# LayerNorm on GpSimd in another form, and a last output tile in three steps: a fused attention and spatial-gating kernel

## The chip, the cores and the metric

The kernel runs on one core of a Trainium2 chip. The metric is the device time of one execution in microseconds. The profile's span, from first to last instruction, is about 1.8 us shorter (span 203.2 in an execution of 204.99 us). Each execution has a state: "slow" if it is over 1.5% above the fastest of the same kernel. That window keeps very different shares of the executions (8 of 22 in experiment 5, 20 of 22 in experiment 9), so medians of all executions stand beside the ratios. Ratios are computed as the mean time of one kernel's fast runs over that of the other's fast runs of the same rounds, so they are not quite the ratio of the medians that I quote.

In the profile PE is TensorE (PEld its weight loads), DVE VectorE, ACT ScalarE, POOL GpSimd, SP SyncE. L326 is line 326 of that kernel's own source, so the same step has other line numbers in other kernels.

## The reference, cut to what matters

```python
# attention in chunks of 64 tokens: x[8, 576, 512]; then the gated block:
h = np.maximum(x @ w_in, 0.0)                       # 512 -> 1024
u, v = h[..., :512], h[..., 512:]
mu = np.mean(v, axis=-1, keepdims=True)
var = np.mean((v - mu) ** 2, axis=-1, keepdims=True)
v_n = (v - mu) / np.sqrt(var + 1e-06)               # <- the change is here
v_s = np.einsum('ts,bsd->btd', w_spatial, v_n) + b_spatial[None, :, None]
out = (u * v_s) @ w_out                             # <- and at the end of this
```

There are 4608 tokens, that is 36 tiles of 128. Four tiles are shared by two batches: their lower 64 rows (the even half) go one way, their upper 64 rows (the odd half) another. `w_spatial` is drawn very small (0.01/576) beside a bias of ones, so the comparison with the reference hardly feels an error in `v_n`.

## The kernel before

Each step is an `op` with an engine, an assumed duration, the ops it waits for and a function that emits the instructions. A list scheduler with its own clock runs through them while the kernel is built and so fixes the order of instructions on every engine. Each engine then works its list in that order.

```python
def rs(n):                       # ScalarE: rstd = exp(-0.5 ln(var + eps)), for one or two tiles
    ...
    nc.scalar.activation(lnv[:, :w], mvs[n][:, :w, 1:2], AF.Ln, bias=eps_sb)
    nc.scalar.activation(rstds[n][:, :w, 0:1], lnv[:, :w], AF.Exp, scale=-0.5)

def nm(n):                       # VectorE: -mean * rstd, the L311 of the profile
    nc.vector.scalar_tensor_tensor(out=rstds[n][:, :w, 1:2], in0=mvs[n][:, :w, 0:1], scalar=-1.0,
                                   in1=rstds[n][:, :w, 0:1], op0=ALU.mult, op1=ALU.mult)

def vnorm(t):                    # GpSimd: v * rstd + (-mean * rstd), L326 (L322 for an even half)
    ...
    nc.gpsimd.tensor_scalar(vn[t], vr, s[:, 0:1], s[:, 1:2], op0=ALU.mult, op1=ALU.add)

def vnorm_o(t):                  # VectorE: the odd half of a shared tile, L331
    nc.vector.tensor_scalar(y[0:64], vr[64:128], s[64:128, 0:1], s[64:128, 1:2],
                            op0=ALU.mult, op1=ALU.add)
...
op(f"nm{n}", DVE_, 0.17, [f"rs{n}"], lambda n=n: nm(n), 1)
op(f"vn{t}", POOL_, 0.80, [f"nm{n}"], lambda t=t: vnorm(t), 0, [("vn", t)])
...
# last tile in two halves, stored from SyncE's queue
n = 2 if t == NT - 1 else 1
...
op(f"st{w}", SP_, 0.62, [f"eo{w}"], lambda t=t, c=c: store(t, c), -200, dma=(SP_, 0.85 / n, f"st{w}*", 128))
```

GpSimd has a second job: it casts the loaded q, k and v from float32 to bfloat16 (L176, L179), and TensorE waits for those casts.

The softmax here doesn't subtract the row's maximum and nothing guards it: scores larger than these inputs give would overflow.

## Time and profile before

| | before |
|---|---|
| executions known at the prediction (us) | 202.41, 206.48, 208.65, and the profiled one, 204.99 |
| span of the profiled execution | 203.2 us |
| TensorE busy / idle | 192.2 / 11.0 us |
| GpSimd busy | 106.7 us (52%) |

GpSimd's three costliest groups are the normalisations and the casts of v and of q (those of k, 16.6 us, are like those of q). Each line gives the count, then busy us and mean ns of one, then idle us just before them:

```profile
L326 POOL TENSOR_SCALAR vn<-v_relu,rstd 128x512 bf16<-128x512 f32 x32 | 24.4, 781 | 28.7 <-DVE rstd L311 22.3
...
L179 POOL CAST vaug<-vf 128x512 bf16<-128x512 f32 x36 | 21.9, 626 | 15.8 <-issue 8.7
...
L176 POOL CAST qb<-qf 128x1024 bf16<-128x1024 f32 x16 | 16.7, 1042 | 20.8 <-DMA qf<-in_q_dram 19.1
```

### The profile page before, as it was taken

What the parts mean: (1) busy time and instruction counts of PE and PEld (TensorE: products, weight loads), DVE (VectorE), ACT (ScalarE), POOL (GpSimd) and SP (SyncE); (2) the same over time, 40 slices, a digit from 0 to 9 for tenths busy, and PEclk for the clock granted to TensorE, in tenths of its full rate; (3) what the DMA queues carried; (4) which work ended last, traced back from release to release, by engine and by line L of the source; (5) the groups of instructions that cost most, each with busy time, mean ns of one, the idle gap of its engine ahead of it and who ended that gap; (6) DMA issues with size and microseconds to landing.
All of it is one profiled execution on the core that took longest, in us unless ns stands there. A gap on an engine that the chain in (4) does not pass through costs nothing.

```text
span 203.2 us, 7600 instructions
## 1 busy us (share of the span) xinstructions
PE 192.2 (95%) x3228; PEld 107.2 (53%) x3228; DVE 127.6 (63%) x337; ACT 115.5 (57%) x209; POOL 106.7 (52%) x155
## 2 busy tenths in 40 slices
PE   7999978989999999999999988999999999999992
PEld 2344434554765556446645634656665446467651
DVE  3226457797746767877776898754477888327330
ACT  2223637867166777976677774574376861640432
POOL 8789394379962375996774995961102222200000
PEclk9999999999999999999999999999999999999999
DMA  5999979999989998999979999871401400212515
GB/s 155 217 311 227 290 202 173 223 271 199 294 209 337 304 298 218 266 293 285 257 190 279 261 240 305 232 197 55 155 5 62 151 2 3 103 74 84 208 52 206
DMA packets 57218, 40.10 MB, mean 197 GB/s; under 512 B 40864, under 2 KB 44384, under 8 KB 57184
## 3 DMA queue, kind: packets, MB, share of 16 engines
q1 hardware_dynamic: 52368, 36.32, 61.5%
q0 software_dynamic: 4816, 3.29, 11.1%
q8 instruction: 25, 0.41, 0.8%
q14 instruction: 9, 0.07, 0.1%
HBM read 32.79 MB, written 9.44 MB: 208 GB/s over the span
## 4 chain that ended last, share of the span: by engine, by line
PE 88%; DVE 3%; DMA 2%; POOL 2%; ACT 2%; issue 1%; SPq 1%; POOLq 0%; ACTq 0%
PE big L352 20%; PE big L280 16%; PE big L376 15%; PE big L337 15%; PE big L390 6%; PE o_ps L231 4%; PE s_ps L194 4%; PE s_ps L216 3%; PE o_ps L245 2%; DMA qf<-in_q_dram 2%; PE big L194 1%; DVE xT L253 1%; PE big L262 1%; POOL qb L176 1%; PE s_ps L192 1%
## 5 line engine op out<-in xcount | busy, mean ns | idle before, releaser
L369 DVE TENSOR_TENSOR gat<-big,uT 128x288 bf16<-128x288 f32 (+8 forms) x96 | 30.2, 351 | 22.6 <-PE big L352 21.2
L352 PE MATMUL big<-wsf,vn 128*128 128x288 bf16 x256 | 40.4, 286 | 0.0
L280 PE MATMUL big<-w_in_sb,xT 128*128 128x512 bf16 x144 | 37.1, 379 | 3.2 <-DVE xT L253 3.1
L326 POOL TENSOR_SCALAR vn<-v_relu,rstd 128x512 bf16<-128x512 f32 x32 | 24.4, 781 | 28.7 <-DVE rstd L311 22.3
L296 DVE BATCH_NORM_STATS2 bst<-v_relu 128x6 f32<-128x512 f32 x36 | 24.9, 690 | 18.8 <-ACT v_relu L287 18.7
L337 PE MATMUL big<-xT,w_in_sb 128*128 128x512 bf16 x144 | 34.6, 380 | 0.0
L376 PE MATMUL big<-w_out_sb,gat 128*128 128x512 bf16 (+2 forms) x164 | 34.4, 376 | 0.0
L287 ACT ACTIVATE v_relu<-big 128x512 f32<-128x512 f32 x35 | 20.9, 598 | 23.8 <-PE big L280 23.0
L382 ACT COPY o_sb<-big 128x512 f32<-128x512 f32 (+1 forms) x30 | 16.9, 571 | 23.6 <-PE big L376 23.6
L179 POOL CAST vaug<-vf 128x512 bf16<-128x512 f32 x36 | 21.9, 626 | 15.8 <-issue 8.7
L221 ACT ACTIVATE eT<-s_ps 128x512 bf16<-128x512 f32 x36 | 21.5, 597 | 15.4 <-PE s_ps L194 8.8
L199 ACT COPY qkT<-s_ps 128x1024 bf16<-128x1024 bf16 x29 | 29.2, 1007 | 1.7 <-PE s_ps L194 1.5
L352 PEld LDWEIGHTS <-vn 128*128 128x128 bf16 x256 | 24.0, 97 | 8.6
L176 POOL CAST qb<-qf 128x1024 bf16<-128x1024 f32 x16 | 16.7, 1042 | 20.8 <-DMA qf<-in_q_dram 19.1
L239 DVE TENSOR_TENSOR x<-o_ps,rz 128x512 bf16<-128x512 f32 x36 | 24.9, 691 | 1.2
L280 PEld LDWEIGHTS <-xT 128*128 128x128 bf16 x144 | 13.1, 97 | 18.2 <-DVE xT L253 5.2
L376 PEld LDWEIGHTS <-gat 128*128 128x128 bf16 (+1 forms) x164 | 13.5, 100 | 14.9 <-issue 1.5
L337 PEld LDWEIGHTS <-w_in_sb 128*128 128x128 bf16 x144 | 13.1, 98 | 14.7
L287 ACT ACTIVATE uT<-big 128x512 bf16<-128x512 f32 x27 | 16.1, 596 | 7.3 <-PE big L337 7.3
L253 DVE COPY xT<-o_ps 128x512 bf16<-128x512 bf16 x36 | 14.6, 406 | 8.3 <-PE o_ps L245 8.3
L390 PE MATMUL big<-warm 128*128 128x512 bf16 x63 | 18.5, 431 | 1.2 <-DVE warm L394 1.2
L352 PE MATMUL big<-wst,tail 65*128 65x288 bf16 x64 | 18.4, 288 | 0.0
(53 smaller groups left out, 208.6 us busy)
## 6 DMA issues: line engine op xcount, KB each, us to landing
out_dram<-o_sb SPq DMA_DIRECT2D x35, 256.0 KB, 2.1
qf<-in_q_dram SPq DMA_DIRECT2D x32, 256.0 KB, 5.2
kf<-in_k_dram SPq DMA_DIRECT2D x32, 256.0 KB, 4.9
vf<-in_v_dram SPq DMA_DIRECT2D x32, 256.0 KB, 6.0
w_in_sb<-in_moe_w_in_dram POOLq DMA_DIRECT2D x2, 512.0 KB, 8.2
vf<-in_v_dram SPq DMA_DIRECT2D x8, 128.0 KB, 5.7
ws_nat<-in_moe_w_spatial_dram POOLq DMA_DIRECT2D x1, 576.0 KB, 9.5
qb<-in_q_dram POOLq DMA_DIRECT2D x16, 32.0 KB, 5.4
```

Of the source, the lines that this page charges most:

```text
L179: CAST[eng](vaug[t % NVB][:, :, 0:64], f32.pop(("v", t)))
L199: nc.scalar.copy(qkT[n], tr_v.rearrange("p b r x -> p b x r"))
L239: nc.vector.tensor_tensor(xs[t], av_v[:, :, :, 0:64], rz.to_broadcast([128, 2, 4, D]), op=ALU.mult)
L280: nc.tensor.matmul(y, xT[g][:, cb, r * 128:(r + 1) * 128], w_in_sb[:, cb, F:], start=(cb == 0), stop=(cb == 3))
L287: nc.scalar.activation(out_, in_, AF.Relu)
L296: nc.vector.bn_stats(bst, relu[t])
L326: nc.gpsimd.tensor_scalar(vn[t], vr, s[:, 0:1], s[:, 1:2], op0=ALU.mult, op1=ALU.add)
L337: nc.tensor.matmul(y, w_in_sb[:, cb, fb * 128:(fb + 1) * 128], xT[g][:, cb, :], start=(cb == 0), stop=(cb == 3))
L352: nc.tensor.matmul(y[:, 0:HS], lhsT, rhs, start=(i == 0), stop=(i == 4))
L369: nc.vector.tensor_tensor(gat[b][:, db, c:c + n], ps["sp", b, half, db][:, o:o + n], uT[g][:, db, r:r + n], op=ALU.mult)
L376: nc.tensor.matmul(y[r0:r0 + n, c], gat[b][:, jb, s:s + n], w_out_sb[:, jb, c], start=(jb == 0), stop=(jb == 3))
L390: nc.tensor.matmul(y, warm[:, 0:128], warm, start=True, stop=True)
```

## The change

The intent is to drop the 20 small VectorE products and one hop in the chain from statistics to normalised tile, by applying (v - mean) * rstd in one instruction, and to shorten the end.

```diff
-        nc.scalar.activation(rstds[n][:, :w, 0:1], lnv[:, :w], AF.Exp, scale=-0.5)
-
-    def nm(n):
-        ...
+        nc.scalar.activation(rstds[n][:, :w], lnv[:, :w], AF.Exp, scale=-0.5)
...
+    def normalise(eng, out_, in_, mean, rstd):
+        eng.tensor_scalar(out_, in_, mean, rstd, op0=ALU.subtract, op1=ALU.mult)
...
-            nc.gpsimd.tensor_scalar(vn[t], vr, s[:, 0:1], s[:, 1:2], op0=ALU.mult, op1=ALU.add)
+            normalise(nc.gpsimd, vn[t], relu[t], mean, rstd)
...      (the even half on GpSimd and the odd half on VectorE likewise)
-            op(f"nm{n}", DVE_, 0.17, [f"rs{n}"], lambda n=n: nm(n), 1)
-            op(f"vn{t}", POOL_, 0.80, [f"nm{n}"], lambda t=t: vnorm(t), 0, [("vn", t)])
+            op(f"vn{t}", POOL_, 0.80, [f"rs{n}"], lambda t=t: vnorm(t), 0, [("vn", t)])
...
+    def cuts(t):
+        return [(0, 256), (256, 384), (384, 512)] if t == NT - 1 else [(0, 512)]
...
+            last = c1 - c0 == 128
+            op(f"st{w}", ACT_ if last else SP_, 0.62, [f"eo{w}"],
+               lambda t=t, c=c, q=nc.scalar if last else nc.sync: store(q, t, c), -200,
+               dma=(ACT_ if last else SP_, 0.85 * m, f"st{w}*", 128))
...      (the test that keeps SyncE's queue from overfilling is moved; alone it changes no order)
```

More of the change, by code (lines that the diff above doesn't have):

```diff
@@ L304, in rs @@
         lnv = stat_pool.tile([128, 2, 1], FP32, name="lnv")
-        rstds[n] = stat_pool.tile([128, 2, 2], FP32, name="rstd")
+        rstds[n] = stat_pool.tile([128, 2, 1], FP32, name="rstd")
         nc.scalar.activation(lnv[:, :w], mvs[n][:, :w, 1:2], AF.Ln, bias=eps_sb)
-        nc.scalar.activation(rstds[n][:, :w, 0:1], lnv[:, :w], AF.Exp, scale=-0.5)
-    def nm(n):
-        w = 1 if PARTS[n][0] == "x" else 2
-        nc.vector.scalar_tensor_tensor(out=rstds[n][:, :w, 1:2], in0=mvs[n][:, :w, 0:1], scalar=-1.0,
-                                       in1=rstds[n][:, :w, 0:1], op0=ALU.mult, op1=ALU.mult)
+        nc.scalar.activation(rstds[n][:, :w], lnv[:, :w], AF.Exp, scale=-0.5)
     def norm_of(t):
         n = part_of(t)
-        return rstds[n][:, t - PARTS[n][1], :]
+        i = t - PARTS[n][1]
+        return mvs[n][:, i, 0:1], rstds[n][:, i, :]
+    def normalise(eng, out_, in_, mean, rstd):
+        eng.tensor_scalar(out_, in_, mean, rstd, op0=ALU.subtract, op1=ALU.mult)
     def vnorm(t):
-        vr, s = relu[t], norm_of(t)
+        mean, rstd = norm_of(t)
         if shared(t):
             y = tails[0][t // 9 % NTB]
-            nc.gpsimd.tensor_scalar(y[0:64], vr[0:64], s[0:64, 0:1], s[0:64, 1:2],
-                                    op0=ALU.mult, op1=ALU.add)
+            normalise(nc.gpsimd, y[0:64], relu[t][0:64], mean[0:64], rstd[0:64])
         else:
             vn[t] = vn_pool.tile([128, F], BF16, name="vn")
-            nc.gpsimd.tensor_scalar(vn[t], vr, s[:, 0:1], s[:, 1:2], op0=ALU.mult, op1=ALU.add)
+            normalise(nc.gpsimd, vn[t], relu[t], mean, rstd)
     def vnorm_o(t):
-        vr, s = relu[t], norm_of(t)
+        mean, rstd = norm_of(t)
         y = tails[1][t // 9 % NTB]
-        nc.vector.tensor_scalar(y[0:64], vr[64:128], s[64:128, 0:1], s[64:128, 1:2],
-                                op0=ALU.mult, op1=ALU.add)
+        normalise(nc.vector, y[0:64], relu[t][64:128], mean[64:128], rstd[64:128])
     def uu(g, fb):
@@ L382, in ev_o, with store @@
         (nc.vector.tensor_copy if eng == "DVE" else nc.scalar.copy)(osb[t][:, c], ps["fin", t, c][:, c])
-    def store(t, c):
-        nc.sync.dma_start(out=out_flat[t * 128:(t + 1) * 128, c], in_=osb[t][:, c])
+    def store(queue, t, c):
+        queue.dma_start(out=out_flat[t * 128:(t + 1) * 128, c], in_=osb[t][:, c])
     def keep_warm():
@@ L512 @@
             op(f"rs{n}", ACT_, 0.45, [f"bn{t}"] + ([] if shared(t) else [f"bn{t + 1}"]), lambda n=n: rs(n), 1)
-            op(f"nm{n}", DVE_, 0.17, [f"rs{n}"], lambda n=n: nm(n), 1)
         if shared(t):
-            op(f"vn{t}", POOL_, 0.80, [f"nm{n}"], lambda t=t: vnorm(t), 0, [("t0", t)])
-            op(f"vo{t}", DVE_, 0.55, [f"nm{n}"], lambda t=t: vnorm_o(t), 2, [("t1", t)])
+            op(f"vn{t}", POOL_, 0.80, [f"rs{n}"], lambda t=t: vnorm(t), 0, [("t0", t)])
+            op(f"vo{t}", DVE_, 0.55, [f"rs{n}"], lambda t=t: vnorm_o(t), 2, [("t1", t)])
             frees("relu", t, [f"vn{t}", f"vo{t}"])
         else:
-            op(f"vn{t}", POOL_, 0.80, [f"nm{n}"], lambda t=t: vnorm(t), 0, [("vn", t)])
+            op(f"vn{t}", POOL_, 0.80, [f"rs{n}"], lambda t=t: vnorm(t), 0, [("vn", t)])
             frees("relu", t, [f"vn{t}"])
@@ L547 @@
         need = sorted({(b, hh) for _, n, b, s in pieces(t) for hh in range(s // HS, (s + n - 1) // HS + 1)})
-        n = 2 if t == NT - 1 else 1
-        for j in range(n):
-            w, c = f"{t}.{j}", slice(j * d_model // n, (j + 1) * d_model // n)
-            op(f"fi{w}", PE_, 0.87 / n, [f"ml{b}{hh}{db}" for b, hh in need for db in range(4)] + ["wlo*"],
+        for j, (c0, c1) in enumerate(cuts(t)):
+            w, c, m = f"{t}.{j}", slice(c0, c1), (c1 - c0) / d_model
+            last = c1 - c0 == 128
+            op(f"fi{w}", PE_, 0.87 * m, [f"ml{b}{hh}{db}" for b, hh in need for db in range(4)] + ["wlo*"],
                lambda t=t, c=c: fin(t, c), 5, [("big", ("fin", w)), ("osb", t)])
-            op(f"eo{w}", EV_, 0.18 + 0.42 / n, [f"fi{w}"], lambda eng, t=t, c=c: ev_o(eng, t, c), 1)
+            op(f"eo{w}", ACT_ if last else EV_, 0.18 + 0.42 * m, [f"fi{w}"],
+               lambda eng=ACT_, t=t, c=c: ev_o(eng, t, c), 1)
             frees("big", ("fin", w), [f"eo{w}"])
-            op(f"st{w}", SP_, 0.62, [f"eo{w}"], lambda t=t, c=c: store(t, c), -200,
-               dma=(SP_, 0.85 / n, f"st{w}*", 128))
-        users["osb", t] = {f"st{t}.{j}*" for j in range(n)}
+            op(f"st{w}", ACT_ if last else SP_, 0.62, [f"eo{w}"],
+               lambda t=t, c=c, q=nc.scalar if last else nc.sync: store(q, t, c), -200,
+               dma=(ACT_ if last else SP_, 0.85 * m, f"st{w}*", 128))
+        users["osb", t] = {f"st{t}.{j}*" for j in range(len(cuts(t)))}
     for g in range(NG):
@@ L561 @@
     for b in range(B):
-        frees("gat", b, [f"fi{t}.{j}" for t in batch_tiles(b) for j in range(2 if t == NT - 1 else 1)])
+        frees("gat", b, [f"fi{t}.{j}" for t in batch_tiles(b) for j in range(len(cuts(t)))])
         sps = [f"sp{b}{half}{db}" for half in (0, 1) for db in range(4)]
@@ L600, in have @@
     def have(x):
-        if x["dma"] and x["dma"][0] == SP_ and sum(r[3] * r[1] / r[4] for r in rings.get(SP_, [])) > RING:
-            return False
         if x["dma"] and x["dma"][0] == POOL_ and len(soft) >= 8:
@@ L668, in choose @@
             return min(c, key=lambda x: (ready_at[x["name"]] + 0.5 * x["pri"]))
-        return min(c, key=lambda x: (x["pri"], ready_at[x["name"]]))
+        x = min(c, key=lambda x: (x["pri"], ready_at[x["name"]]))
+        if eng == SP_ and sum(r[3] * r[1] / r[4] for r in rings.get(SP_, [])) > RING:
+            return None
+        return x
     with tc.manual_schedule(engines={getattr(mybir.EngineType, e) for e in
```

## The prediction

> **What bounds the kernel now.** I read the page's busy shares first, then TensorE's waits, then its gaps stage by stage, then the timeline around the largest one. The page:
>
> ```profile
> span 203.2 us, 7600 instructions
> ...
> PE 192.2 (95%) x3228; PEld 107.2 (53%) x3228; DVE 127.6 (63%) x337; ACT 115.5 (57%) x209; POOL 106.7 (52%) x155
> ...
> PE   7999978989999999999999988999999999999992
> ```
>
> TensorE is the bound: 192.2 of 203.2 us, so all idle time is 11.0 us. By the table of busy time per stage it lies so: 0 to 10 us 1.6 us, 10 to 25 us none (filled with 63 warming matmuls, 18.5 us in the whole run, that do nothing useful), 25 to 40 us 2.4 us, 40 to 120 us 1.2 us, 120 to 140 us 1.9 us, 140 to 195 us none, and 4.0 us at the end, after the last matmul. A change that takes no work off TensorE can only win from these pieces. The list of TensorE's waits gives the ones inside:
>
> ```profile
> PE big L280 <- DVE xT L253: 3.1, 5, 1.9
> PE s_ps L216 <- issue: 0.9, 1, 0.9
> PE s_ps L194 <- POOL qb L176: 0.7, 1, 0.7
> ```
>
> The columns are total, times, longest. So the longest wait inside the run is one of 1.9 us, for VectorE's copy of the transposed attention output (L253). No matmul of the spatial product (L352), which reads the normalised tiles, has idle time in front of it: the normalisation's own latency is hidden. It matters only as something that stands in the way of others on VectorE and GpSimd.
>
> The instruction that the change removes is L311, the product -mean * rstd. The view of that line (min/median/max ns):
>
> ```profile
> L311 DVE SCALAR_TENSOR_TENSOR rstd<-mv,rstd x20: 129/156/2871, 23.2 to 175.3; 128x2 f32<-128x2 f32 x16, 128x1 f32<-128x1 f32 x4
> ```
>
> A two-element operation with a median of 0.156 us took 2.87 us once. The timeline there (start, us), VectorE, then GpSimd, then TensorE:
>
> ```profile
> 118.16 2.87 DVE L311 SCALAR_TENSOR_TENSOR rstd<-mv,rstd 128x1 f32<-128x1 f32 x1
> 121.07 0.55 DVE L331 TENSOR_SCALAR tail<-v_relu,rstd 64x512 bf16<-64x512 f32 x1
> 121.65 0.69 DVE L296 BATCH_NORM_STATS2 bst<-v_relu 128x6 f32<-128x512 f32 x1
> 122.38 0.18 DVE L300 BATCH_NORM_AGGREGATE mv<-bst 128x2 f32<-128x6 f32 x1
> 122.48 0.39 DVE L253 COPY xT<-o_ps 128x512 bf16<-128x512 bf16 x1
> ```
>
> ```profile
> 117.83 0.73 POOL L179 CAST vaug<-vf 128x512 bf16<-128x512 f32 x1
> 118.44 1.60 POOL L326 TENSOR_SCALAR vn<-v_relu,rstd 128x512 bf16<-128x512 f32 x2
> 119.91 1.10 POOL L176 CAST qb<-qf 128x1024 bf16<-128x1024 f32 x1
> 121.14 1.04 POOL L322 TENSOR_SCALAR tail<-v_relu,rstd 64x512 bf16<-64x512 f32 x1
> ```
>
> ```profile
> 122.93 1.04 PE L280 MATMUL big<-w_in_sb,xT 128*128 128x512 bf16 x4 [1.86 <-DVE xT L253]
> ```
>
> GpSimd works without a pause from 117.83 to 121.01; L311 starts at 118.16 and ends at 121.03, when GpSimd pauses, because its next instruction needs L311. Only then do VectorE's queued L331, L296, L300 and L253 run, and TensorE stands for 1.86 us. The chain of waits puts this stretch down to ScalarE and VectorE and doesn't name L311. Four more of the 20 are long: 0.72 (89.59), 0.59 (81.03), 0.36 (43.07) and 0.21 us (51.78); the first three end within 0.03 us of the end of a GpSimd cast. L311's 7.0 us in all are thus some 3.1 us of work (20 x 0.156) and 3.9 us of blocking.
>
> **What the Trainium skill says.** "SBUF — State Buffer", § Who interferes with whom: a VectorE instruction with two SBUF inputs contends with a GpSimd instruction that reads SBUF, and the later one blocks fully. L311 reads mean and rstd, both in SBUF, and the trace above agrees (2.87 us under three GpSimd groups); it shows that the block can last over several GpSimd instructions. "GPSIMD Engine Reference", § 3.1: 512 elements at 1.8 cycles each take 768 ns. L326's median of 768 ns is just that. The page has no line on subtract-then-multiply against multiply-then-add; no run here shows it yet. "DMA: Bandwidth & Descriptors", § Anatomy of one DMA: a fixed cost of some 2.0 us whatever the size (for GpSimd's kind of queue). The output stores here, from SyncE's queue, agree: 1.9 to 2.1 us to landing, for 256 KB and for 128 KB.
>
> **The change, part by part.**
>
> 1. Product gone. 20 VectorE instructions, 7.0 us, vanish; VectorE is 63% busy, so most of it is beside the path. On the path: the gap of 1.86 us at 121 us, which I take as wholly removed (without L311 the copy of 122.48 would have been through at about 120.2, before TensorE ran dry at 121.07), and at 43.07, where the chain does name L311 with 0.27 us ahead of a 0.33 us gap. Together 2.1 us. The other three blocked ones stand beside a busy TensorE: nothing.
>
> 2. GpSimd starts its normalisation one hop earlier. L326 waited 22.3 us for L311, but 21.0 us of that are the four waits after 150 us (6.23, 4.69, 6.26, 3.75), where GpSimd has next to nothing else; 0. At 33 us L311 sat 0.4 us behind a VectorE activation, GpSimd's normalisation of 1.52 us then stood ahead of the query cast, and TensorE waited 0.74 us for that cast. Some 0.4 us could come back there: I count 0.2.
>
> 3. Price of the new form. It is still one instruction with two per-partition scalars; I keep 0.77 us for 32 and VectorE's 0.55 us for 4. Zero.
>
> 4. Order. The kernel computes its own instruction order with an internal clock, so removing a product moves everything after about 23 us. Building both shows: the work is the same, 512+128 query and key transposes, 576 scores, 144 + 144 for the first product, 320 spatial; 62 warming matmuls for 63; the order is the same up to the last warming and different after it. In the new order spatial products start earlier among the first activations. The other gaps (25 to 40 us: 2.4 us; 40 to 120 us: 0.9 without the one named) are redrawn, which can give or take about 1 us: 0 in the middle. The rewriting of the store-queue test moves nothing: built alone it gives the order of before on all five engines.
>
> 5. The end. Before: copies of 256 columns at 198.89 and 199.24, last store issued at 199.95:
>
> ```profile
> 199.24 0.37 ACT L382 COPY o_sb<-big 128x256 f32<-128x256 f32 x1
> ...
> 199.95 0.41 SPq L385 DMA_DIRECT2D out_dram<-o_sb  x1
> ```
>
> It lands 2.0 us later, and the span ends 1.25 us after that. The build shows that ScalarE now does copies of 256, 128 and 128 columns and only then issues both small stores. From 585 ns for 512 columns and 372 for 256, a copy of 128 is estimated at 0.27 us. The copies would end at 199.26 + 2 x 0.27 = 199.8 instead of 199.61; the hop to SyncE (199.61 to 199.95) goes, but the first small store's issue, 0.33 to 0.41 us on SyncE, stands ahead of the last. The last issue starts at about 200.2, 0.2 later, and lands up to 0.1 faster. Sum +0.1 us.
>
> Sum: -2.1 - 0.2 + 0 + 0 + 0.1 = -2.2 us of span.
>
> **The starting point** is uncertain by more than that: four executions of before are 202.41, 204.99 (profiled, span 203.2), 206.48 and 208.65. Their middle is (204.99 + 206.48) / 2 = 205.7. Less 2.2 is 203.5; as an old stall may come back elsewhere I say 203.8.
>
> **Rivals.** (a) The new order has a stall of its own. For: VectorE still has four halves of shared tiles (L331), one of which took 1.18 us for a median 0.55 with GpSimd busy, and GpSimd is nearly full in much of the first 130 us. Against: four instead of 24 candidates. Time about 205.5. (b) Subtract then multiply is slower on GpSimd. [...]At +0.2 us each, 36 x 0.2 = 7 us of GpSimd, of which three quarters (27 of the 36 start before 150 us) fall where it also feeds the casts; perhaps 1.5 us on the path: again 205 to 206. Against: the present duration is what the page gives for an ordinary loop. (c) The redrawn order is lucky in 25 to 40 us too and 1 to 2 us more are saved: 202. (d) The blocked stretch at 118 us is a matter of chance between executions; then its removal makes the spread of times smaller more than it moves the fastest ones: a median of 204, the fastest near 202.
>
> **Range and chances.** Half of the 6 us spread of before either way covers the doubt of level, the order adds 1 us: 200.5 to 207.5. 2% is 4.1 us, nearly all the idle time inside the run plus luck; faster by that has 0.2. Slower needs a new stall of over 6 us: 0.07. Within 2%: 0.73.
>
> **What would show it right or wrong.** Right: no VectorE instruction of a few elements over 1 us; TensorE busy for the same 192 us, idle 8 to 9.5 us, with no gap near 1.9 us for L253's copy; GpSimd's normalisation at 0.76 to 0.80 us; the end still 4 us after the last matmul. Wrong: normalisations of 0.9 us or more (step 3), a TensorE gap over 1 us in another place (step 4), an end, after the last matmul, shorter than 3.7 us or longer than 4.4 (step 5).

## More of the kernel before

TensorE is the bound, and GpSimd looks like an engine with half of its time free. The page's slices (40 equal slices of 5.1 us, busy share in tenths) say how that half is spread:

```profile
POOL 8789394379962375996774995961102222200000
PEclk9999999999999999999999999999999999999999
```

In the first 27 slices, in which inputs are still loaded and cast, GpSimd is full in several and rarely under a third; the free time is mostly at the end. The second row is the granted TensorE clock: full throughout.

A normalisation of 781 ns is shorter than a query cast of 1042 ns.

## The result, and the profile after

The kernel after takes 216.99 us (median of 4, 216.02 to 217.66, all fast), against 205.8 us before (median of 4, of which the two fast ones are 202.41 and 205.11). The ratio of fast runs is 1.0646 (95% interval 1.0507 to 1.0784): slower, and outside the predicted range. The page after:

```profile
span 215.3 us, 7602 instructions
...
PE 194.4 (90%) x3231; PEld 108.7 (51%) x3231; DVE 123.2 (57%) x318; ACT 116.0 (54%) x209; POOL 152.8 (71%) x155
...
POOL 8498496889995639999999999999514493730000
PEclk9999988969999999999999999999999999999999
...
L316 POOL TENSOR_SCALAR vn<-v_relu,mv,rstd 128x512 bf16<-128x512 f32 x32 | 66.3, 2086 | 23.0 <-ACT rstd L307 12.6
```

GpSimd went from 106.7 to 152.8 us with the same 155 instructions. The last line says why: a normalisation now takes 2086 ns where it took 781. 32 x (2086 - 781) ns is 41.8 us; the four even halves, now in another group of the same line, went from 3.6 to 9.0 us. VectorE shows no such loss in its shortest run; its view of the odd half, before and then after, min/median/max:

```profile
L331 DVE TENSOR_SCALAR tail<-v_relu,rstd x4: 547/548/1180, 45.2 to 162.9; 64x512 bf16<-64x512 f32 x4
```

```profile
L316 DVE TENSOR_SCALAR tail<-v_relu,mv,rstd x4: 547/815/890, 43.6 to 174.9; 64x512 bf16<-64x512 f32 x4
```

The shortest is 547 ns in both. The medians differ (548 and 815 ns), but this instruction is stretched now and then whatever its operations are: with multiply, add it takes 547/654/3726 ns in experiment 2.

In GpSimd's row the slices from the 16th to the 28th are now all full (a 9 is 90% or more). TensorE's waits for GpSimd, before and then after (total, times, longest):

```profile
PE s_ps L194 <- POOL qb L176: 0.7, 1, 0.7
PE big L194 <- POOL qb L176: 0.4, 1, 0.4
```

```profile
PE s_ps L194 <- POOL qb L176: 6.4, 5, 2.1
PE o_ps L231 <- POOL vaug L179: 3.2, 2, 1.6
PE s_ps L194 <- POOL kb L176: 1.8, 1, 1.8
PE big L350 <- POOL tail L316: 1.6, 1, 1.6
```

TensorE waits 13.0 us for GpSimd, where the list before had 1.1. Most of it is not for normalised tiles but for casts that stand behind them in GpSimd's list. One such place, GpSimd and then TensorE:

```profile
36.02 4.13 POOL L316 TENSOR_SCALAR vn<-v_relu,mv,rstd 128x512 bf16<-128x512 f32 x2 [1.77 <-PE big L335]
40.11 1.03 POOL L176 CAST qb<-qf 128x1024 bf16<-128x1024 f32 x1
```

```profile
41.19 0.41 PE L194 MATMUL s_ps<-permq,qb 64*128 64x64 bf16 x16 [1.75 <-POOL qb L176]
```

Two normalisations hold GpSimd for 4.13 us, the query cast comes after them, and TensorE, which needs the cast, stands for 1.75 us.

By stage, TensorE's idle time (stage length less its busy time):

| stage (us) | before | after |
|---|---|---|
| 0 to 10 | 1.6 | 1.2 |
| 10 to 25 | 0 | 1.6 |
| 25 to 40 | 2.4 | 3.3 |
| 40 to 60 | 0.5 | 3.5 |
| 60 to 120 | 0.7 | 5.1 |
| 120 to 140 | 1.9 | 2.1 |
| after the last matmul | 4.0 | 4.1 |
| sum | 11.0 | 20.9 |

The other 2.2 us of the 12.1 us of span are busy time: 194.4 for 192.2 us. Four matmuls were added (the last tile's third step) and one warming one dropped, and the granted clock was 0.83 in 30 to 40 and in 40 to 50 us, where it had been 1.00. The 1.6 us in 10 to 25 us come before the first normalisation (24.50), so the slow form is not their cause. In this execution GpSimd waited for a load of v until 10.60, where it was there before 8.76 in the execution of before.

The end, in which the prediction wanted 4.1 us, has 4.1: the last matmul ends at 211.2 of 215.3 us.

```profile
211.16 0.46 ACT L384 COPY o_sb<-big 128x128 f32<-128x128 f32 x2
...
211.47 0.91 ACTq L387 DMA_DIRECT2D out_dram<-o_sb  x2
```

### The profile page after: what moved, and what is told of

It is laid out like the page before. It is cut to its first block, busy times and chain, and to the rows that moved or that the text cites.

```text
span 215.3 us, 7602 instructions
## 1 busy us (share of the span) xinstructions
PE 194.4 (90%) x3231; PEld 108.7 (51%) x3231; DVE 123.2 (57%) x318; ACT 116.0 (54%) x209; POOL 152.8 (71%) x155
## 4 chain that ended last, share of the span: by engine, by line
PE 61%; POOL 14%; DMA 11%; issue 5%; SPq 5%; ACT 1%; DVE 0%; POOLq 0%; ACTq 0%
PE big L350 16%; PE big L378 13%; PE big L335 10%; PE big L280 10%; DMA vf<-in_v_dram 5%; SPq L164 4%; DMA qf<-in_q_dram 4%; PE s_ps L194 3%; POOL vn L316 3%; PE o_ps L231 3%; POOL vaug L179 3%; DMA qb<-in_q_dram 3%; POOL qb L176 2%; PE big L392 2%; POOL qb L159 2%
## 5 line engine op out<-in xcount | busy, mean ns | idle before, releaser
L316 POOL TENSOR_SCALAR vn<-v_relu,mv,rstd 128x512 bf16<-128x512 f32 x32 | 66.3, 2086 | 23.0 <-ACT rstd L307 12.6
L296 DVE BATCH_NORM_STATS2 bst<-v_relu 128x6 f32<-128x512 f32 x36 | 24.9, 692 | 27.1 <-ACT v_relu L287 27.1
L280 PE MATMUL big<-w_in_sb,xT 128*128 128x512 bf16 x144 | 38.7, 393 | 0.5 <-DVE xT L253 0.5
L287 ACT ACTIVATE v_relu<-big 128x512 f32<-128x512 f32 x36 | 21.5, 597 | 27.3 <-PE big L280 27.2
L335 PE MATMUL big<-xT,w_in_sb 128*128 128x512 bf16 x144 | 35.1, 380 | 0.0
L378 PE MATMUL big<-w_out_sb,gat 128*128 128x512 bf16 (+3 forms) x168 | 34.2, 371 | 0.0
L384 ACT COPY o_sb<-big 128x512 f32<-128x512 f32 (+2 forms) x31 | 17.0, 560 | 22.0 <-PE big L378 22.0
L280 PEld LDWEIGHTS <-xT 128*128 128x128 bf16 x144 | 13.9, 99 | 15.7 <-issue 1.1
L287 ACT ACTIVATE uT<-big 128x512 bf16<-128x512 f32 x24 | 14.3, 597 | 5.8 <-PE big L335 5.7
L253 DVE COPY xT<-o_ps 128x512 bf16<-128x512 bf16 x36 | 14.7, 407 | 4.2 <-PE o_ps L245 4.2
```

Of the source, the lines that this page charges most:

```text
L280: nc.tensor.matmul(y, xT[g][:, cb, r * 128:(r + 1) * 128], w_in_sb[:, cb, F:], start=(cb == 0), stop=(cb == 3))
L287: nc.scalar.activation(out_, in_, AF.Relu)
L296: nc.vector.bn_stats(bst, relu[t])
L316: eng.tensor_scalar(out_, in_, mean, rstd, op0=ALU.subtract, op1=ALU.mult)
L335: nc.tensor.matmul(y, w_in_sb[:, cb, fb * 128:(fb + 1) * 128], xT[g][:, cb, :], start=(cb == 0), stop=(cb == 3))
L378: nc.tensor.matmul(y[r0:r0 + n, c], gat[b][:, jb, s:s + n], w_out_sb[:, jb, c], start=(jb == 0), stop=(jb == 3))
```

## The experiments

The theory after this reading: on GpSimd the pair subtract, multiply is slow, that is the whole loss, and it acts through the casts. Rivals: not the operations but the operands (two scalars from two tiles) are slow; the new order hurts by itself; the last stores hurt.

**1. Eleven forms of the instruction in one kernel.** The kernel after, its 32 full normalisations dealt out over eleven forms on eleven source lines; results wrong.

```diff
-            normalise(nc.gpsimd, vn[t], relu[t], mean, rstd)
+            pair(t, vn[t], relu[t], mean, rstd)     # eleven forms in turn, for example
+            ts(o, i, r, m, op0=ALU.mult, op1=ALU.add)
+            ts(o, i, m, var, op0=ALU.subtract, op1=ALU.mult)   # both scalars from one tile
```

> The kernel after, its 32 full GpSimd normalisations spread over eleven forms, each on its own source line (results wrong on purpose). Theory A (the pair of operations decides): subtract-then-multiply 2.07 us, multiply-then-add 0.77 us with mean and rstd in two tiles as with mean and variance in one. Rival B (two scalars from two tiles, or reading the mean straight from the aggregate, decide): multiply-then-add with the two tiles also takes about 2.07 us, and subtract-then-multiply with both scalars in one tile 0.77 us. Rival C (subtract alone is slow): a single subtract and multiply-then-subtract take 2 us too, add-then-multiply 0.77 us. Rival D (only multiply-then-add is fast): all other two-operation forms take about 2.07 us.

Each line's view, min/median/max ns, in the order subtract-multiply, multiply-add, add-multiply, add-add, multiply alone, and subtract-multiply with both scalars from one tile:

```profile
L323 POOL TENSOR_SCALAR vn<-v_relu,mv,rstd x3: 2067/2071/2072, 23.7 to 139.7; 128x512 bf16<-128x512 f32 x3
...
L325 POOL TENSOR_SCALAR vn<-v_relu,rstd,mv x3: 758/768/843, 25.8 to 141.7; 128x512 bf16<-128x512 f32 x3
...
L327 POOL TENSOR_SCALAR vn<-v_relu,mv,rstd x3: 761/767/825, 33.8 to 155.3; 128x512 bf16<-128x512 f32 x3
...
L333 POOL TENSOR_SCALAR vn<-v_relu,mv,rstd x3: 2097/2097/2157, 50.9 to 163.2; 128x512 bf16<-128x512 f32 x3
...
L339 POOL TENSOR_SCALAR vn<-v_relu,rstd x3: 1559/1562/1652, 73.4 to 177.5; 128x512 bf16<-128x512 f32 x3
...
L341 POOL TENSOR_SCALAR vn<-v_relu,mv x3: 2062/2066/2077, 74.9 to 179.0; 128x512 bf16<-128x512 f32 x3
```

All medians, for 128x512 from float32 to bfloat16:

| form on GpSimd | ns |
|---|---|
| multiply, add | 768 (scalars from one tile: 757) |
| add, multiply | 767 |
| multiply, multiply | 771 |
| subtract, multiply | 2071 (from one tile: 2066) |
| multiply, subtract | 2081 |
| subtract, add | 2077 |
| add, add | 2097 |
| subtract alone | 1561 |
| multiply alone | 1562 |

So the operands don't matter (rival B falls) and the operations do: the four figures of theory A came. C and D, which say which operations are slow, don't fit: add-then-add is as slow as anything with a subtraction, two pairs besides multiply-then-add are fast, and one operation alone takes twice as long as three of the pairs. Three pairs are fast (four of the eleven forms); the other seven forms aren't. Why just these, the runs don't say.

**2. The fast pair in the order of after.** One line; every instruction stays in its place on every engine (both kernels' instruction lists agree but for operands).

```diff
-        eng.tensor_scalar(out_, in_, mean, rstd, op0=ALU.subtract, op1=ALU.mult)
+        eng.tensor_scalar(out_, in_, rstd, mean, op0=ALU.mult, op1=ALU.add)      # wrong on purpose
```

> The kernel after, every instruction in the same order, but the normalisation multiplies and then adds (rstd first, then mean: wrong result on purpose). Theory A: GpSimd normalisations back at 0.77 us, GpSimd busy about 106 us, and the time drops from 217 to what was predicted, 203 to 205 us; then all the loss is the slow pair. If order, missing product or the last stores cost something: 207 us or more. Rival B: stays at 217 us.

GpSimd's normalisation is back at 778 ns and its busy time at 106.8 us. Fast runs are 0.9994 of before (0.9937 to 1.005): same. So in fast runs the pair accounts for the loss. But the predicted gain isn't there either, and 14 of its 20 executions were over 207 us where 4 of 23 of before in these rounds were (medians 208.77 and 204.97). Those are slow runs, and I don't explain a difference that only they show; that this order falls into them more often stays as a finding.

**3. The slow pair in the order of before.** The product is still made, the odd half on VectorE and the last stores are as before.

```diff
-            nc.gpsimd.tensor_scalar(vn[t], vr, s[:, 0:1], s[:, 1:2], op0=ALU.mult, op1=ALU.add)
+            nc.gpsimd.tensor_scalar(vn[t], vr, mean_of(t), s[:, 0:1], op0=ALU.subtract, op1=ALU.mult)
...      (the even half likewise; mean_of gives the mean as bn_aggr left it)
```

> The kernel before, every instruction in the same order and the product still made, but GpSimd subtracts the mean and multiplies by rstd (right result). Theory A: GpSimd normalisations at 2.07 us, GpSimd busy about 153 us, time 214 to 219 us, as slow as the kernel after although order and last stores are those of before. If the new order is what hurts: 207 us or less.

It takes 218.06 us (217.03 to 226.64), ratio 1.0684 (1.0574 to 1.0795). The run's own label is "unclear"; three of its four executions are fast, and the interval is far from 1. GpSimd is busy 153.2 us, and TensorE's waits for query casts are 12.2 us, where they were 1.1. Nothing differs from before but the pair of operations and the tile that the mean is read from, which by experiment 1 costs nothing. So the pair is sufficient: neither the new order nor the last stores are needed for the loss.

**4. The slow pair, planned as slow.** The kernel after with the duration in its planning set right.

```diff
-            op(f"vn{t}", POOL_, 0.80, [f"rs{n}"], lambda t=t: vnorm(t), 0, [("vn", t)])
+            op(f"vn{t}", POOL_, 2.10, [f"rs{n}"], lambda t=t: vnorm(t), 0, [("vn", t)])
...      (the even half likewise)
```

> The kernel after, with only the duration that the kernel's own planning of the order assumes for a GpSimd normalisation set from 0.80 to 2.10. If a bad plan makes the loss (casts queued behind a normalisation that lasts longer than planned): a good part comes back, 208 to 212 us. If GpSimd's capacity in the first 150 us makes it: 214 us or more.

209.42 us (208.28 to 210.01), ratio 1.0263 (1.0149 to 1.0376; label "unclear", since the interval spans 2%): with GpSimd as busy as in the kernel after (153.2 us), more than half of the excess over before is gone (from 6.5% to 2.6%). TensorE's waits for GpSimd in this profile are 1.6, 0.9 and 0.4 us, 2.9 in all for 13.0. So much of the loss was a list of instructions made for 0.80 us and run at 2.09, with casts queued behind normalisations. Where the remaining 2.6% sits is not shown: the new duration redraws the whole order, and direct waits for GpSimd are only part of it. The stage from 25 to 40 us has the most idle time, 5.1 us. One of its waits, 2.2 us for the load of `w_spatial`, is indirect: GpSimd issued that load at 30.11 us, behind a normalisation and casts (27.97 before).

**5. The last stores alone.** The kernel before with the diff's `cuts`, `fin` and `store` only; nothing else moves.

> The kernel before with only the last output tile in three steps and its two last stores from ScalarE's queue; all else in the order of before. By the prediction's step 5 the time from the last matmul to the end goes from 4.0 to 4.1 us and the time stays within 0.3% of before. Rival: if the three steps cost more, the end is over 4.5 us.

204.82 us for 204.07 (medians), ratio 0.9976 (0.9934 to 1.0019): same. The end is 4.1 us after the last matmul.

**6. A product that GpSimd cannot hold up.** Still in the order of before: the prediction's step 1 put the gap of 1.86 us at 121 us down to the second SBUF input of L311.

```diff
-        nc.vector.scalar_tensor_tensor(out=rstds[n][:, :w, 1:2], in0=mvs[n][:, :w, 0:1], scalar=-1.0,
-                                       in1=rstds[n][:, :w, 0:1], op0=ALU.mult, op1=ALU.mult)
+        for i in range(w):
+            nc.vector.tensor_scalar(rstds[n][:, i, 1:2], mvs[n][:, i, 0:1], rstds[n][:, i, 0:1], -1.0,
+                                    op0=ALU.mult, op1=ALU.mult)
```

> The kernel before in its own order, the product made by one or two VectorE instructions with a single SBUF tensor input each (the second factor is a per-partition scalar) in place of one with two. If the second tensor input is what lets GpSimd hold it up: no such instruction over 0.4 us, no TensorE wait of 1.9 us near 121 us, and 0 to 2 us faster than before (mean 203.5 to 205). Rival (any small VectorE instruction on SBUF is held up): some of them still over 0.5 us and no gain.

All 36 take 181 to 215 ns, also where GpSimd is at work: this agrees with the block by the second SBUF input (the kind of instruction changed along with the inputs). But the time is the same, ratio 1.0024 (0.9961 to 1.0086), and TensorE still waits 1.56 us for L253's copy at 123.78. The next instruction on VectorE, the odd half, took 2.91 us in its place.

**7. No product at all, in the order of before.** The plan keeps its slot, nothing is emitted, GpSimd and VectorE multiply by rstd and add the mean.

```diff
     def nm(n):
-        nc.vector.scalar_tensor_tensor(...)
+        pass
```

> The kernel before in its own order with no product at all and no tail change; GpSimd multiplies by rstd and adds the mean (wrong on purpose, the fast pair). It is the prediction's steps 1 and 2 without a new order. If these steps are right: 1 to 2.5 us faster than before. If the new order is what keeps the kernel after with the fast pair at 203 to 212 us: this one shows fewer executions over 207 us than that one. Rival (the product was hidden all along): equal to before within 0.5%.

205.62 us for 204.07 (medians), ratio 1.0059 (1.002 to 1.0099): no gain, if anything a loss. VectorE near 118 us and TensorE after it:

```profile
117.88 3.23 DVE L331 TENSOR_SCALAR tail<-v_relu,rstd,mv 64x512 bf16<-64x512 f32 x1
```

```profile
122.48 1.68 PE L280 MATMUL big<-w_in_sb,xT 128*128 128x512 bf16 x4 [1.86 <-DVE xT L253]
```

There is no L311 any more, and a gap of 1.86 us is there again. The odd half, 547 ns when free, holds VectorE for 3.23 us; GpSimd works in that stretch without a pause, from 115.39 to 121.59. (This profile and that of experiment 6 fell in executions of the slow state; the stretched instruction and the gap after it are read from the trace, not from their times.)

Is this gap in every execution of an order that allows it? It isn't. The profile of experiment 5 has the order of before, L311 included, at the same place:

```profile
116.16 0.83 DVE L311 SCALAR_TENSOR_TENSOR rstd<-mv,rstd 128x1 f32<-128x1 f32 x1
```

There GpSimd was already in the last of its three groups of work when L311 started (in the profile of before it was in the first), and L311 was held up for 0.83 us in all, not 2.87. The matmuls behind it (L280, at 118.89 in that execution) started without a wait; TensorE's longest wait for L253's copy in the whole run was 0.5 us.

**8. A mended kernel.** The kernel after with the negated mean made on ScalarE, so that GpSimd can add and multiply; right result.

```diff
+        nc.scalar.mul(negm[n][:, :w], mvs[n][:, :w, 0:1], -1.0)
...      (the planned duration of rs goes from 0.45 to 0.65, so the order is drawn again)
-        eng.tensor_scalar(out_, in_, mean, rstd, op0=ALU.subtract, op1=ALU.mult)
+        eng.tensor_scalar(out_, in_, negm, rstd, op0=ALU.add, op1=ALU.mult)      # names shortened
```

> A mended kernel, right result: the negated mean made by a small ScalarE instruction, GpSimd adds it and multiplies by rstd (a pair that took 0.77 us), no VectorE product, last stores as in the kernel after. If the slow pair is the whole loss: 203 to 206 us, GpSimd busy about 107 us. If the order of the kernel after hurts too: 206 to 210 us, as with multiply-then-add in that order.

205.79 us, ratio to before 1.0085 (1.0051 to 1.0118). All but 0.9% of the loss is mended by swapping a subtraction for an addition, at the price of a small ScalarE instruction (187 ns, 20 times) and of one more order. The tile that comes out holds the same values as with the subtraction, at 772 ns (median) for 2072, so it isn't the values that are slow. A gain over the kernel before isn't there.

**9. Nothing on VectorE that GpSimd can hold up.** Experiment 6 with the odd half on ScalarE; order of before.

```diff
-        nc.vector.tensor_scalar(y[0:64], vr[64:128], s[64:128, 0:1], s[64:128, 1:2],
-                                op0=ALU.mult, op1=ALU.add)
+        nc.scalar.activation(y[0:64], vr[64:128], AF.Identity, scale=s[64:128, 0:1], bias=s[64:128, 1:2])
```

> The kernel before in its own order, with the one-input product of before_nolock and the odd half of a shared tile normalised on ScalarE in place of VectorE, so that no VectorE instruction is left that GpSimd held up in the traces so far. If the hold-up that the prediction saw (1.86 us near 121 us) only moved to that odd half in before_nolock and before_noproduct: no VectorE instruction stretched, no TensorE wait over 1 us near 120 us, and a mean 1 to 2 us below before_nolock, so 0 to 1% faster than before. Rival (TensorE would wait there anyway, for another reason): the wait of 1.5 to 1.9 us is still there and the time equals before.

203.05 us for 204.65 (medians), ratio 0.9961 (0.9934 to 0.9989): 0.4% faster, the only kernel here whose interval lies below 1. TensorE's longest wait for L253's copy is no longer 1.9 us:

```profile
PE big L280 <- DVE xT L253: 1.8, 5, 0.7
```

TensorE has no idle time at all from 120 to 140 us. And none of its 22 executions was over 207 us (201.94 to 205.93), where 9 of 43 of before were. That its profile lacks the gap says less than it seems to, since the profile of experiment 5 lacks it too, with L311 in place. I did not try it with the three-step end, which by experiment 5 would change nothing that these rounds can see.

**10. The mended kernel with the odd half on ScalarE.** Experiment 8 plus `scale=rstd, bias=-mean*rstd` on ScalarE, with the four products there too.

> The mended kernel (negated mean on ScalarE, add then multiply on GpSimd, last stores as in the kernel after) with the odd half on ScalarE as well. If the hold-up on VectorE is what costs the mended kernel its 0.8%: equal to or up to 1% faster than before. Rival (its order is simply no better): 0.5 to 1% slower than before, as without this.

Fast runs are 1.0028 of before (0.9987 to 1.0068): same. 10 of 22 executions were over 207 us. So in the order that the planning makes without the VectorE product, freedom from the hold-up isn't enough for a gain. The traces name one place, though not its cause. In this profile (slow) and in that of experiment 8 (fast), TensorE's longest wait is for a query cast near 55 us, 3.06 and 2.15 us, and the cast itself stood for its load. From experiment 8, GpSimd and then TensorE:

```profile
53.32 1.04 POOL L176 CAST qb<-qf 128x1024 bf16<-128x1024 f32 x1 [2.80 <-DMA qf<-in_q_dram]
```

```profile
54.42 0.41 PE L194 MATMUL s_ps<-permq,qb 64*128 64x64 bf16 x16 [2.15 <-POOL qb L176]
```

From 40 to 60 us TensorE is idle for 3.5 and 3.3 us there, and for 0.5 us before and 0.4 in experiment 9. No run tests whether this wait makes the difference in time.

## Why the prediction was wrong

**Step 3, the price of the new form ("Zero"), is the step that failed.** It kept 0.77 us because the form stayed one instruction with two scalars. Measured: 2.07 us (median; mean 2.09), 1.3 us more, 36 times. Experiment 3 shows that this alone makes the whole loss, and experiment 2 that the loss goes with it. The danger was named as rival (b), with the right direction and both sizes wrong: 0.2 us each was 1.3, and 1.5 us on the path was some 12. What set it aside was that L326's 768 ns is just the figure of the "GPSIMD Engine Reference", § 3.1: a coincidence taken as evidence. The page calls that figure the best case of a tight, unrolled loop, and in experiment 1 seven of eleven forms are slower. Nor is it that a subtraction is slow as such: add-then-add takes 2097 ns. VectorE's 0.55 us, the other half of step 3, held for the shortest run (547 ns).

**Why 1.3 us each cost 12 us in all.** The prediction had read that the normalisation's own latency is hidden, and that it matters as something that stands in the way of others. That was right, and its consequence was drawn only for 0.2 us. TensorE's waits for GpSimd grew from 1.1 to 13.0 us. Of the 13.0, 1.6 come before the first normalisation and 1.6 are for a normalised tile itself; the other 9.8 are for casts. Each of these casts follows a normalisation, or two, in GpSimd's list. By experiment 4 more than half of the loss goes when the planning knows the true duration; the rest comes with 46 us more of work on GpSimd, but by which waits is not shown.

**Step 1, the product gone (-2.1 us), failed as well, by rivals (a) and (d).** That L311 was blocked holds: with one SBUF tensor input the product is never held up (experiment 6). What was wrong is that removing L311 removes the gap from every execution. First, rival (a): the odd half L331 stood right behind it, was exposed to GpSimd in the same stretch, and was held up in its place: 2.91 us in experiment 6, 3.23 in experiment 7 and 3.73 in experiment 2, with gaps of 1.56, 1.86 and 1.94 us. The Trainium skill's "SBUF — State Buffer", § Who interferes with whom, counts a one-input `tensor_scalar` among those that can contend, in a 2-port mode; its "VectorE: DVE Perf Modes", § The perf-mode tier table, gives such an instruction from float32 in SBUF up to 2x. The free 547 ns for 512 columns are shorter than the 690 ns of bn_stats (L296) for as many, which would fit a faster mode; no run shows the mode itself. The prediction had the L331 of 1.18 us before its eyes and weighed it as 4 candidates against 24; what counts is which instruction comes next in the same stretch.

Second, rival (d): the gap is partly a matter of chance between executions. With L311 in place it is 1.86 us in the profile of before and absent in that of experiment 5. With both candidates out of VectorE's way (experiment 9) the fastest execution hardly moves (201.94 for 202.05 us), the median does (203.05 for 204.65), and none is over 207 us: much what (d) foresaw. In fast runs this is worth 0.4%, not the 1% of step 1. That the shorter tail comes from the hold-up is likely, not shown.

**Step 2 (-0.2)** can't be told apart: experiment 7 contains it and shows no gain.

**Step 4, the order (0).** In fast runs 0 is what experiment 2 shows (0.9994). Not foreseen: that order was over 207 us in 14 of 20 executions.

**Step 5, the end (+0.1)** was right: 4.0 became 4.1 us. (The "1.9 to 2.1 us to landing" in the prediction are the least and the median of the stores; the longest was 6.1 us.) Inside it, copies of 128 columns took 0.23 us each (0.46 for two) for the estimated 0.27, and the last issue starts 0.7 us after the last matmul as it did before, for the expected 0.2 us later.

## What to carry to other kernels

Before rewriting an algebraically equal form on GpSimd, time that form there: an instruction of the same shape with another pair of operations took 2.7 times as long, and VectorE gave no warning, as its shortest run is 547 ns with either pair. When an instruction is found held up, look at what is queued behind it that can be held up in the same way, since removing only the first can move the wait on. Before a gap in one trace is booked as a gain, look for it in a second execution of the same order. And when an off-path engine serves two purposes in order, a longer instruction for the idle purpose is paid by the busy one; tell a static planner the measured duration at least.

## What the Trainium skill lacked or had wrong

- "GPSIMD Engine Reference", § 3.1: its 1.8 cycles per element (768 ns for 512) is called the best case of an unrolled loop. Here 767 to 771 ns is what three pairs of `tensor_scalar` take (multiply-add, add-multiply, multiply-multiply); four other pairs take 2071 to 2097 ns and a single operation 1561 ns. The page has no list of this, and a single operation being slower than a pair is nothing that its count of operations per element leads one to expect.
- "SBUF — State Buffer", § Summary: rules for kernel authors: the later instruction blocks "until the first finishes". Here a VectorE instruction could wait over several GpSimd instructions in a row: 2.87 us (L311 before, until GpSimd paused) and 3.23 us (L331 in experiment 7). It need not: the L311 of 0.72 us (89.59 before) ended with one cast, though another followed at once.
- The same page lets a one-input `tensor_scalar` contend with GpSimd in a 2-port mode only, and no page says whether one of a single column, with a per-partition scalar, takes such a mode. Here 36 of them took 181 to 215 ns each and were never held up (experiment 6).
